# Storing weight gradients 1 MB at a time from common buffers in a four-pass attention kernel

## The chip, the cores and the metric

The kernel runs on one core of a Trainium2 chip. The metric is the device time of one execution in microseconds. Most kernels here were run five or six times, in rounds that alternate with runs of the kernel before on the same chip. A verdict of faster or slower needs 2%.

The engines by their names in the profile: PE (matrix multiply), PEld (its weight loads), DVE (vector), ACT (scalar), POOL (it issues the stores here), SP (it issues the loads here; "SPq" is its queue).

## The reference, cut to what matters

Two transformer layers are applied to one token, with the same weights used twice, and the gradients of all inputs are returned:

```python
x = x + attention(layernorm(x), k_cache, v_cache, wq, wo)   # 32 heads in 4 groups, 65,536 keys of 128
x = x + mlp(layernorm(x), w1, b1, w2, b2)                   # 1024 -> 3584 -> 1024, squared relu
# ... both once more; then the vector-Jacobian product with grad_out
```

The caches of K and V are 67 MB each. They are read four times (two forward passes, two backward passes), and gradients of the same size are written in the fourth pass. Each of the four weight gradients is a product of rank 2 (one term from each layer), 7.3 or 8.4 MB in bf16, 31 MB together. They too are made in the fourth pass, as background work.

## The kernel before

All loads and the K/V gradient stores use 11 common buffers ("slots") of 8 KB per partition, 1 MB each, reused in the order in which they are freed:

```python
FREE = deque(range(NSLOT))                     # NSLOT = 11
class Slot:
    def __init__(self):
        self.i = FREE.popleft()
        self.t = slotp.tile([P, BLK], BF, tag="slot%d" % self.i)     # BLK = 32 * 128
    def free(self):
        FREE.append(self.i)
```

The SP queue is in order: if the next load wants a buffer that is still in use, all loads behind it wait too. A pass is a pipeline over blocks of 8 key columns, and after each step the background gets a turn. First come the urgent generators (products of weight rows with a vector, which read 1 MB weight slabs through slots), then the normal ones (the weight gradients), which catch up with their schedule in a loop:

```python
def step(self, i):
    while self.urgent:
        if next(self.urgent[0][1], "end") == "end":
            self.urgent.popleft(); continue
        return
    want = self.total * (i - 2) / self.steps
    while self.normal and self.done < want:      # may run many times in one step
        ... next(self.normal[0]) ...; self.done += 1

def g_outer(pool, out_dram, nA, nB, a_cols, b_cols, c0=0):
    ...
    for ka in range(an):
        og = pool.tile([P, 8 * P], BF, name="og", tag="og", bufs=3)       # three buffers of 256 KB
        for n0 in range(0, bn * P, 512):
            pg = ps_gg()
            nc.tensor.matmul(pg[:, 0:nn], lhsT=ra[...], rhs=rb[...], start=True, stop=True)   # rank 2
            evac(og[:, n0:n0 + nn], pg[:, 0:nn], kind="f32")              # ACT or DVE
        nc.gpsimd.dma_start(out=out_dram[k * P:(k + 1) * P, ...], in_=og[...])
        yield
```

The tile `E` (64 KB per partition) holds the exponentials of both layers. The fourth pass reads it for the last time, from the last group to the first, and inside a group from the last column to the first.

## Time and profile before

| | before |
|---|---|
| median of 3 runs | 2097.63 us (2091.03 to 2101.38) |
| profiled run, span | 2109.1 us (2110.86 us as timed, longer than each of the three) |
| bytes moved | 803.55 MB, 381 GB/s on average |
| fourth pass, from its first V transpose (1265.6 us) to the end | 843.5 us |
| DMA idle in the fourth pass, by slices of 10 us from its start to the end of the span | 78.0 us |

From the page of the profile of before: the span; the granted TensorE clock in 40 slices of the span, in tenths of full speed; the busy share of the DMA engines in tenths; and GB/s in each slice.

```profile
span 2109.1 us, 69960 instructions
...
PEclk9999999579999987999999997859888888896897
DMA  9999999889999998999999996969989999999996
GB/s 381 418 416 417 417 415 403 315 323 412 408 411 418 415 369 322 375 412 416 415 419 416 384 328 233 370 233 395 390 338 422 404 394 371 420 389 375 386 411 280
```

For most of the first three passes DMA is at 9 tenths or more and moves 410 to 420 GB/s. Dips mark the dense stages between the passes. In the fourth pass (from the 25th slice) the rate falls to 233 twice and later to 338, 371 and 375, and the clock row dips with it.

Stretches of 10 us of before. The columns are the stretch, then busy us and the number of instructions of PE, PEld, DVE, ACT and POOL, then granted clock, DMA share and GB/s.

```profile
1360.00:1370.00 10.00, 7.38 (x62) 4.07 (x61) 5.35 (x18) 4.18 (x7) 2.16 (x4) 0.80 1.01 386
1370.00:1380.00 10.00, 5.16 (x35) 2.38 (x35) 4.17 (x8) 2.83 (x5) 1.62 (x3) 0.50 0.69 279
...
1390.00:1400.00 10.00, 6.58 (x32) 2.42 (x31) 4.31 (x13) 3.96 (x8) 1.62 (x3) 0.50 0.42 159
1400.00:1410.00 10.00, 10.00 (x53) 3.50 (x52) 3.99 (x7) 6.44 (x13) 1.86 (x4) 0.50 0.64 236
1410.00:1420.00 10.00, 10.00 (x59) 3.85 (x60) 6.00 (x11) 6.67 (x12) 1.37 (x3) 0.50 0.60 246
...
1450.00:1460.00 10.00, 9.34 (x146) 6.14 (x147) 8.98 (x18) 8.14 (x16) 2.15 (x4) 1.00 1.02 426
...
1470.00:1480.00 10.00, 8.46 (x98) 4.40 (x95) 6.28 (x12) 5.51 (x11) 1.61 (x3) 1.00 1.02 427
```

The stretches at 1450 and 1470 show what the pass can do: DMA share 1.02 and 426 GB/s. In the four slices shown between 1370 and 1420 DMA is at 0.42 to 0.69. PE is cold there (0.50): even where it is busy all the time (10.00) it gets through fewer than 60 matmuls in 10 us, against 146 at 1450. (Part of that is the mix: a burst of gradients brings more matmuls of 512 columns.)

From the list of waits of before over the fourth pass (us in total, times, longest us): ACT and DVE wait for a gradient store to land so that one of its three buffers comes free, and DVE once waits for a weight slab.

```profile
ACT og L144 <- DMA out_dram<-og: 64.6, 23, 7.0
DVE og L147 <- DMA out_dram<-og: 60.1, 21, 7.8
...
DVE mv_junk L345 <- DMA slot_32475<-in_A_wq_dram: 6.8, 1, 6.8
```

The chain of waits of before after 1500 us, summed by line:

```profile
by line: DMA out_dram<-og 22.6%; PE ps_gg L881 14.3%; PE ps_tr L818 12.3%; PE ps_gg L925 5.8%; PE ps_sc L837 5.1%; PE ps_acc L867 4.8%; issue 3.9%; PE ps_tr L849 3.2%; DMA slot_32475<-in_A_wq_dram 2.2%; DMA slot_42058<-in_A_k_cache_dram 2.0
```

Over a fifth of this chain is a gradient store ("out_dram<-og"). A store on the chain is not all loss, because DMA is also full much of that time.

### The profile page before, as it was taken

Reading aid. Unit: us, or ns where it says so; the run is one execution under the profiler, and the core shown is the slowest. Engines: PE = TensorE matmul, PEld = TensorE weight load, DVE = VectorE, ACT = ScalarE, POOL = GpSimd, SP = SyncE. Lnnn points to the kernel's source line nnn. Section 1 sums busy time; section 2 is a strip of 40 time slices with the busy share of each in tenths; the row PEclk is TensorE's granted clock in tenths of the full one; section 3 lists DMA queues with packets and bytes.
Section 4 is the critical chain, followed back from the end, with each engine's and each line's share of the span. In section 5 each row is a group of like instructions: output and inputs, shape, how many; then the busy total and the mean of one; then the engine's idle time right before and its main releaser. Section 6 shows DMA issues by size and latency. Waiting matters only on the chain.

```text
span 2109.1 us, 69960 instructions
## 1 busy us (share of the span) xinstructions
PE 1747.5 (83%) x31172; PEld 1368.0 (65%) x31172; DVE 1184.0 (56%) x2435; ACT 1121.9 (53%) x2029; POOL 139.6 (7%) x278
## 2 busy tenths in 40 slices
PE   6878787788888877888787797889788989888997
PEld 6777776787777776777677785535445554454553
DVE  3445444244444443834434367758667777686785
ACT  3545545144445452624334356647667766676775
POOL 0000000000000000000000000112111211111111
PEclk9999999579999987999999997859888888896897
DMA  9999999889999998999999996969989999999996
GB/s 381 418 416 417 417 415 403 315 323 412 408 411 418 415 369 322 375 412 416 415 419 416 384 328 233 370 233 395 390 338 422 404 394 371 420 389 375 386 411 280
DMA packets 148807, 803.55 MB, mean 381 GB/s; under 512 B 13964, under 2 KB 13978, under 8 KB 69274
## 3 DMA queue, kind: packets, MB, share of 16 engines
q1 hardware_dynamic: 120282, 633.39, 75.6%
q0 software_dynamic: 28224, 165.70, 19.3%
q8 instruction: 243, 3.98, 0.7%
q14 instruction: 58, 0.48, 0.1%
HBM read 633.35 MB, written 165.69 MB: 379 GB/s over the span
## 4 chain that ended last, share of the span: by engine, by line
PE 41%; DMA 34%; ACT 13%; DVE 8%; issue 3%; SPq 0%; ACTq 0%; POOL 0%; POOLq 0%; DVEq 0%
DMA out_dram<-og 9%; PE ps_gg L881 6%; PE ps_tr L566 6%; PE ps_tr L818 5%; ACT E L623 5%; PE ps_sc L584 4%; PE ps_tr L373 3%; PE ps_acc L650 3%; ACT kt L144 3%; DVE kt L147 3%; PE ps_gg L925 2%; PE ps_sc L837 2%; PE ps_acc L867 2%; PE ps_tr L849 1%; PE ps_bg L389 1%
## 5 line engine op out<-in xcount | busy, mean ns | idle before, releaser
L147 DVE COPY kt<-ps_tr 128x1024 bf16<-128x1024 bf16 x680 | 458.9, 687 | 342.7 <-PE ps_tr L566 157.5
L144 ACT COPY kt<-ps_tr 128x1024 bf16<-128x1024 bf16 x344 | 347.9, 1024 | 468.9 <-PE ps_tr L566 252.5
L584 PE MATMUL ps_sc<-L_qpad,kt 128*128 128x64 bf16 (+7 forms) x4096 | 196.0, 195 | 54.1 <-DVE kt L147 41.8
L584 PEld LDWEIGHTS <-kt 128*128 128x128 bf16 x4096 | 158.0, 100 | 73.4 <-DVE kt L147 50.3
L623 ACT ACTIVATE E<-S_sb,L_negm 128x128 bf16<-128x128 f32 x256 | 150.7, 988 | 26.5 <-DVE L_negm L619 26.5
L623 ACT ACTIVATION_READ_ACCUMULATOR E<-S_sb,L_negm 128x1 f32 x256 | 123.3, 482 | 0.0
L144 ACT CAST og<-ps_gg 128x512 bf16<-128x512 f32 x135 | 78.5, 593 | 79.6 <-DMA out_dram<-og 64.6
L837 PE MATMUL ps_sc<-DOB,kt 128*128 128x64 bf16 (+3 forms) x2048 | 119.6, 201 | 0.0
L147 DVE CAST og<-ps_gg 128x512 bf16<-128x512 f32 x105 | 72.0, 689 | 78.2 <-DMA out_dram<-og 60.1
L925 PE MATMUL ps_gg<-rowb,rowa 2*128 2x512 bf16 x240 | 93.0, 434 | 27.2 <-ACT og L144 17.6
L837 PEld LDWEIGHTS <-kt 128*128 128x128 bf16 x2048 | 95.4, 104 | 30.8 <-issue 29.0
L144 ACT COPY wt<-ps_tr 128x1024 bf16<-128x1024 bf16 (+1 forms) x60 | 57.6, 966 | 105.9 <-PE ps_tr L373 103.3
L729 PE MATMUL ps_sc<-dOpad,kt 128*128 128x64 bf16 (+7 forms) x2048 | 99.1, 194 | 15.5 <-ACT kt L144 11.8
L729 PEld LDWEIGHTS <-kt 128*128 128x128 bf16 x2048 | 76.5, 99 | 32.0 <-ACT kt L144 22.3
L589 DVE TENSOR_REDUCE pm_all<-S_sb 128x8 f32<-128x512 f32 x64 | 43.9, 686 | 91.7 <-ACT S_sb L588 91.6
L147 DVE COPY wt<-ps_tr 128x1024 bf16<-128x1024 bf16 (+1 forms) x92 | 59.7, 662 | 58.8 <-PE ps_tr L373 57.4
L881 PEld LDWEIGHTS <-xt 64*128 64x128 bf16 x1024 | 45.4, 95 | 65.3 <-issue 43.5
L928 POOL DMA_DIRECT2D out_dram<-og x124 | 67.3, 543 | 242.1 <-ACT og L144 104.7
L588 ACT COPY S_sb<-ps_sc 128x512 f32<-128x512 f32 x64 | 37.7, 589 | 82.6 <-PE ps_sc L584 82.4
L351 ACT ACTIVATE mv_t<-mv_t 128x1024 bf16<-128x1024 bf16 x56 | 59.3, 1060 | 24.6 <-DVE mv_t L350 24.5
L144 ACT COPY xt<-ps_tr 128x512 bf16<-128x512 bf16 x113 | 62.5, 596 | 11.0 <-PE ps_tr L849 10.4
L772 POOL COPY F_28535<-L_fw 128x128 f32<-128x128 f32 x2 | 0.6, 291 | 785.7 <-ACT L_fw L671 785.7
(2141 smaller groups left out, 3830.6 us busy)
## 6 DMA issues: line engine op xcount, KB each, us to landing
out_dram<-og POOLq DMA_DIRECT2D x116, 256.0 KB, 9.4
slot_171<-in_A_wq_dram SPq DMA_DIRECT2D x1, 1024.0 KB, 5.1
slot_205<-in_A_wq_dram SPq DMA_DIRECT2D x1, 1024.0 KB, 7.4
slot_245<-in_A_k_cache_dram SPq DMA_DIRECT2D x1, 1024.0 KB, 9.3
slot_292<-in_A_wq_dram SPq DMA_DIRECT2D x1, 1024.0 KB, 10.4
slot_329<-in_A_k_cache_dram SPq DMA_DIRECT2D x1, 1024.0 KB
slot_404<-in_A_wq_dram SPq DMA_DIRECT2D x1, 1024.0 KB
slot_441<-in_A_k_cache_dram SPq DMA_DIRECT2D x1, 1024.0 KB, 15.6
```

Source lines behind the costliest of these rows:

```text
L144: nc.scalar.copy(out=out, in_=in_)
L147: nc.vector.tensor_copy(out=out, in_=in_)
L373: nc.tensor.transpose(pt[:, i, :], slab[:, (q * w + i) * P:(q * w + i + 1) * P], ident_b[:, :])
L566: nc.tensor.transpose(pt[:, i, :], kb8[:, i, :], ident_b[:, :])
L584: nc.tensor.matmul(state["ps_s"][:, s:s + w, :].rearrange("p a b -> p (a b)"), lhsT=kt[:, i, :], rhs=L["qpad"][:, g, 0:w, :].rearrange("p ...
L623: nc.scalar.activation(out=E[:, g, c0:c0 + SU, L["lr"].start + h], in_=S[:, h, :], func=ACTF.Exp, bias=negm[:, g, su, h:h + 1], scale=SCAL ...
L729: nc.tensor.matmul(state["ps_dp"][:, s:s + w, :].rearrange("p a b -> p (a b)"), lhsT=vt[:, i, :], rhs=dOpad[:, g, 0:w, :].rearrange("p a b ...
L818: nc.tensor.transpose(pt[:, i, :], vb8[:, i, :], ident_b[:, :])
L837: nc.tensor.matmul(state["ps_dp"][:, s:s + w, :].rearrange("p a b -> p (a b)"), lhsT=vt[:, i, :], rhs=DOB[:, g, 0:w, :].rearrange("p a b - ...
L881: nc.tensor.matmul(pgs[h][:, :], lhsT=xt[t][64 * h:64 * h + 64, j1 // 8 + m, :], rhs=gg[64 * h:64 * h + 64, :, :].rearrange("p a b -> p (a ...
L925: nc.tensor.matmul(pg[:, 0:nn], lhsT=ra[:, ka * P:(ka + 1) * P], rhs=rb[:, n0:n0 + nn], start=True, stop=True)
L928: nc.gpsimd.dma_start(out=out_dram[k * P:(k + 1) * P, c0 + b0 * P:c0 + (b0 + bn) * P], in_=og[:, 0:bn * P])
```

## The change

The intent: gradients leave in 1 MB stores from the common buffers, at most one background step per pipeline step; halves of E become buffers once the fourth pass has used them; weight slabs are issued five steps before their use; a buffer whose store was just issued is "held back": it goes seven steps further back in the order of reuse; and memory is split as 12 buffers and 6 transposed weight tiles instead of 11 and 7.

```diff
-    NSLOT = 11
-    NWT = 7
+    STORE_STEPS = 7
+    WAIT_STEPS = 5
+    NSLOT = 12
+    NWT = 6
...
-            self.i = FREE.popleft()
+            self.i = heappop(FREE)[1]
...
-        def free(self):
-            FREE.append(self.i)
+        def free(self, stored=False):
+            NOW["step"] += 0.01
+            heappush(FREE, (NOW["step"] + (STORE_STEPS if stored else 0), self.i))
+    def add_slot(pool, tag):
+        SLOTS.append((pool, tag)); ...; heappush(FREE, (NOW["step"], len(SLOTS) - 1))
... # weight rows: the slab is issued by the for, then five steps pass
         for kc, slab in slab_it:
+            if kc % 4 == 0:
+                for _ in range(WAIT_STEPS if PS["pass4"] else 0):
+                    yield "wait"
... # background step: urgent "wait" lets normal work run; one normal step at most
+                if r == "wait":
+                    break
...
                     self.done += 1
+                    return
... # E in eight tiles; after its last use each is a buffer
+    def E_done(g, c0, n):
+        if c0 % EH == 0 and EH * R2 == BLK:
+            add_slot(epool, "E%d_%d" % (g, c0 // EH))
... # gradients
-                    og = pool.tile([P, 8 * P], BF, name="og", tag="og", bufs=3)
+            sl = Slot()
+            og = sl.t[:, :].rearrange("p (j n) -> p j n", j=4)
+            for j in range(4):
+                for n0 in range(0, 1024, 512):
+                    rank2(og[:, j, n0:n0 + 512], ra[:, bass.ds(j, P, step=4)], rb[:, n0:n0 + 512])
+                if j < 3:
+                    yield
+            nc.gpsimd.dma_start(out=out_dram[...].rearrange("(p j) n -> p j n", j=4), in_=og)
+            sl.free(stored=True)
```

The gradient of w1 (out_6) has its own form with rows of 7 KB, also one slot for each store. The gradient of wq still goes out in rows of 2 KB. The change also makes the gradient of wo before that of w1.

More of the change, by code (lines that the diff above doesn't have):

```diff
@@ L2 @@
 from collections import deque
+from heapq import heappush, heappop
 import concourse.bass as bass
@@ L211 @@
     BLK = J * DH
-    FREE = deque(range(NSLOT))
+    SLOTS = [(slotp, "slot%d" % i) for i in range(NSLOT)]
+    FREE = [(0, i) for i in range(NSLOT)]
+    NOW = {"step": 0}
     class Slot:
         def __init__(self):
-            self.i = FREE.popleft()
-            self.t = slotp.tile([P, BLK], BF, name="slot%d" % self.i, tag="slot%d" % self.i)
-        def free(self):
-            FREE.append(self.i)
+            self.i = heappop(FREE)[1]
+            pool, tag = SLOTS[self.i]
+            self.t = pool.tile([P, BLK], BF, name="slot", tag=tag)
+        def free(self, stored=False):
+            NOW["step"] += 0.01
+            heappush(FREE, (NOW["step"] + (STORE_STEPS if stored else 0), self.i))
+    def add_slot(pool, tag):
+        SLOTS.append((pool, tag))
+        NOW["step"] += 0.01
+        heappush(FREE, (NOW["step"], len(SLOTS) - 1))
     def kv_views(ap):
@@ L315, in bcast_vec @@
         nc.vector.tensor_copy(out=rows[0:nj, :], in_=pt[:, :])
-        vbc = pool.tile([P, nj * P], BF, name=tag, tag=tag)
+        vbc = pool.tile([P, nj * P], BF, name=tag, tag=tag, bufs=1)
         for j0 in range(0, nj, 4):
@@ L333, in g_rowdots @@
         n = nj * P
-        vbc = bcast_vec(vcol, nj, mvs, "vbc")
         y = vec.tile([P, nk], F32, name=name)
         nc.gpsimd.memset(y[:], 0.0)
-        yield
+        vbc = None
         L = load
         for kc, slab in slab_it:
+            if kc % 4 == 0:
+                for _ in range(WAIT_STEPS if PS["pass4"] else 0):
+                    yield "wait"
+            if vbc is None:
+                vbc = bcast_vec(vcol, nj, mvs, "vbc")
+                yield
             a = (L["dve"] + 0.10 + n * 0.00105, L["act"])
@@ L437, in step @@
             while self.urgent:
-                if next(self.urgent[0][1], "end") == "end":
+                r = next(self.urgent[0][1], "end")
+                if r == "end":
                     self.urgent.popleft()
                     continue
+                if r == "wait":
+                    break
                 return
-            want = self.total * (i - 2) / self.steps
-            while self.normal and self.done < want:
+            while self.normal and self.done < self.total * (i - 2) / self.steps:
                 if next(self.normal[0], "end") == "end":
@@ L468, in pipeline @@
             bg.step(i)
+            NOW["step"] += 1
     def new_layer(name, lay):
@@ L482, in new_layer, with E @@
         return L
-    E = epool.tile([P, G, C, R2], BF, name="E")
+    EH = max(SU, C // 2)
+    ETILE = {}
+    for g in range(G):
+        for h in range(C // EH):
+            ETILE[(g, h)] = epool.tile([P, EH * R2], BF, name="E", tag="E%d_%d" % (g, h))
+    def E(g, c0, n):
+        h, c = divmod(c0, EH)
+        return ETILE[(g, h)][:, :].rearrange("p (c r) -> p c r", r=R2)[:, c:c + n, :]
+    def E_done(g, c0, n):
+        if c0 % EH == 0 and EH * R2 == BLK:
+            add_slot(epool, "E%d_%d" % (g, c0 // EH))
     def gsl(g):
@@ L622, in stats @@
             for h in range(R):
-                nc.scalar.activation(out=E[:, g, c0:c0 + SU, L["lr"].start + h], in_=S[:, h, :], func=ACTF.Exp,
+                nc.scalar.activation(out=E(g, c0, SU)[:, :, L["lr"].start + h], in_=S[:, h, :], func=ACTF.Exp,
                                      bias=negm[:, g, su, h:h + 1], scale=SCALE, accum_out=rs[:, h:h + 1])
@@ L649, in v8 @@
                 w = min(8, (su + 1) * SU - c)
-                nc.tensor.matmul(ps_o[:, 0:w, :], lhsT=vb8[:, i, :], rhs=E[:, g, c:c + w, lr],
+                nc.tensor.matmul(ps_o[:, 0:w, :], lhsT=vb8[:, i, :], rhs=E(g, c, w)[:, :, lr],
                                  start=(c % SU == 0), stop=(c % SU == SU - 1), skip_group_check=True)
@@ L734, in vS @@
                 nc.vector.tensor_tensor(out=dsT[:, :, :], in0=state["ps_dp"][:, :, :],
-                                        in1=E[:, g, c0:c0 + HB, L["lr"]], op=ALU.mult)
+                                        in1=E(g, c0, HB)[:, :, L["lr"]], op=ALU.mult)
                 add_load(dve=0.7)
@@ L842, in vS @@
                 X = dspool.tile([P, J, R2], BF, name="X", tag="X")
-                nc.vector.tensor_tensor(out=X[:, :, :], in0=ps_dp[:, :, :], in1=E[:, g, c0:c0 + J, :], op=ALU.mult)
+                nc.vector.tensor_tensor(out=X[:, :, :], in0=ps_dp[:, :, :], in1=E(g, c0, J), op=ALU.mult)
                 add_load(dve=0.13 + J * R2 * 0.00105)
                 xt = []
-                for src in (X[:, :, :], E[:, g, c0:c0 + J, :]):
+                for src in (X[:, :, :], E(g, c0, J)):
                     pt2 = ps_tr()
@@ L852, in vS @@
                     xt.append(xx)
+                E_done(g, c0, J)
                 state[("X", g, c0 // J)] = (X, xt)
@@ L888, in k8 @@
                 nc.gpsimd.dma_start(out=(GVv if t else GKv)[g][b], in_=stg)
-                state.pop("st").free()
+                state.pop("st").free(stored=True)
             if c8 == sulast[(g, su)]:
@@ L896, in attn_bwd4, with rows2 @@
         pipeline(items, [(vT, 0), (vS, TLEAD), (k8, B4_LAG)], bg)
-    def rows2(pool, cols, j0, jn, tag):
-        cc = pool.tile([P, 8, 2], BF, name="r2_cc", tag="r2_cc", bufs=2)
+    def rows2(cols, j0, jn, rows):
+        cc = tmp.tile([P, 4, 2], BF, name="r2_cc")
         for l in range(2):
             nc.vector.tensor_copy(out=cc[:, 0:jn, l], in_=cols[l][:, j0:j0 + jn])
-        rows = pool.tile([2, 8 * P], BF, name=tag, tag=tag)
-        for k0 in range(0, jn, 4):
-            kn = min(4, jn - k0)
-            pg = ps_gg()
-            for jj in range(kn):
-                nc.tensor.matmul(pg[0:2, jj * P:(jj + 1) * P], lhsT=cc[:, k0 + jj, :], rhs=ident_b[:, :], start=True, stop=True)
-            evac(rows[0:2, k0 * P:(k0 + kn) * P], pg[0:2, 0:kn * P], kind="f32")
-        return rows
@@ L912, in g_outer @@
-    def g_outer(pool, out_dram, nA, nB, a_cols, b_cols, c0=0):
-        for b0 in range(0, nB, 8):
-            bn = min(8, nB - b0)
-            rb = rows2(pool, b_cols, b0, bn, "rowb")
-            for a0 in range(0, nA, 8):
-                an = min(8, nA - a0)
-                ra = rows2(pool, a_cols, a0, an, "rowa")
-                yield
-                for ka in range(an):
-                    og = pool.tile([P, 8 * P], BF, name="og", tag="og", bufs=3)
-                    for n0 in range(0, bn * P, 512):
-                        nn = min(512, bn * P - n0)
-                        pg = ps_gg()
-                        nc.tensor.matmul(pg[:, 0:nn], lhsT=ra[:, ka * P:(ka + 1) * P], rhs=rb[:, n0:n0 + nn], start=True, stop=True)
-                        evac(og[:, n0:n0 + nn], pg[:, 0:nn], kind="f32")
-                    k = a0 + ka
-                    nc.gpsimd.dma_start(out=out_dram[k * P:(k + 1) * P, c0 + b0 * P:c0 + (b0 + bn) * P], in_=og[:, 0:bn * P])
-                    yield
@@ L931, in n_outer, with rank2 @@
-    def n_outer(nA, nB):
-        return (nA + -(-nA // 8)) * -(-nB // 8)
+        pg = ps_gg()
+        for jj in range(jn):
+            nc.tensor.matmul(pg[0:2, jj * P:(jj + 1) * P], lhsT=cc[:, jj, :], rhs=ident_b[:, :], start=True, stop=True)
+        evac(rows, pg[0:2, 0:jn * P], kind="f32")
+    def rank2(out, ra, rb):
+        pg = ps_gg()
+        n = out.shape[-1]
+        nc.tensor.matmul(pg[:, 0:n], lhsT=ra, rhs=rb, start=True, stop=True)
+        evac(out, pg[:, 0:n], kind="f32")
+    def g_outer(pool, out_dram, nA, nB, a_cols, b_cols, c0=0):
+        rb = pool.tile([2, 8 * P], BF, name="rowb", tag="rowb")
+        for k in range(0, nB, 4):
+            rows2(b_cols, k, 4, rb[0:2, k * P:(k + 4) * P])
+            yield
+        for a0 in range(0, nA, 4):
+            ra = pool.tile([2, 4 * P], BF, name="rowa", tag="rowa", bufs=2)
+            rows2(a_cols, a0, 4, ra[0:2, :])
+            yield
+            sl = Slot()
[4 more added lines that the diff above has]
+                if j < 3:
+                    yield
+            nc.gpsimd.dma_start(out=out_dram[a0 * P:(a0 + 4) * P, c0:c0 + 1024].rearrange("(p j) n -> p j n", j=4), in_=og)
+            sl.free(stored=True)
+            yield
@@ new lines, in g_outer_wide @@
+    def g_outer_wide(pool, out_dram, nA, nB, a_cols, b_cols):
+        rsl = Slot()
+        rb = rsl.t
+        for k in range(0, nB, 4):
+            rows2(b_cols, k, 4, rb[0:2, k * P:(k + 4) * P])
+            yield
+        for a in range(nA):
+            if a % 4 == 0:
+                ra = pool.tile([2, 4 * P], BF, name="rowa", tag="rowa", bufs=2)
+                rows2(a_cols, a, 4, ra[0:2, :])
+                yield
+            sl = Slot()
+            for n0 in range(0, nB * P, 512):
+                rank2(sl.t[:, n0:n0 + 512], ra[:, (a % 4) * P:(a % 4 + 1) * P], rb[0:2, n0:n0 + 512])
+                if n0 % 1024 == 512:
+                    yield
+            nc.gpsimd.dma_start(out=out_dram[a * P:(a + 1) * P, :], in_=sl.t[:, 0:nB * P])
+            sl.free(stored=True)
+            yield
+        rsl.free()
@@ L935, with n_outer @@
+    def n_outer(nA, nB, wide=False):
+        return nB // 4 + nA // 4 + nA * (-(-nB // 8)) if wide else nB // 4 + nA // 4 * 5
     psA_stack = ExitStack()
@@ L1113 @@
     bg.normal.append(g_outer(bgpool, out_8, FC, DC, [L4["g"], L2["g"]], [gx, dx2]))
-    bg.normal.append(g_outer(bgpool, out_6, DC, FC, [L4["n"], L2["n"]], [dh4, dh2]))
     bg.normal.append(g_outer(bgpool, out_5, HQ, DC, [L3["oT"], L1["oT"]], [dx3, dx1]))
-    bg.total = n_outer(FC, DC) + n_outer(DC, FC) + n_outer(HQ, DC) + (G - 1) * n_outer(DC, DC)
+    bg.normal.append(g_outer_wide(bgpool, out_6, DC, FC, [L4["n"], L2["n"]], [dh4, dh2]))
+    bg.total = n_outer(FC, DC) + n_outer(DC, FC, True) + n_outer(HQ, DC) + (G - 1) * n_outer(DC, DC)
     bg.steps = len(ITEMS[3]) - 4
```

## The prediction

> **What bounds it now.** By stretches of 10 us, the first three passes over the caches are bound by DMA: between the dense stages its share is 1.01, at 412 to 418 GB/s; the change hardly touches them. The fourth pass (1280 to 2109 us) moves 306 MB in 830 us, 369 GB/s. Its 24 clean slices (granted clock 1.0, DMA 0.99 or more, PE over 9 of 10 us) move 415 GB/s and run 133 matmuls per 10 us; at those rates its 306 MB need 738 us and its 8,419 recorded matmuls 631 us. So DMA is the floor there, and 90 us are lost:
>
> 1. Idle DMA: the shares sum to 771 us of 830. 21 us are lost between 1370 and 1430, some 20 us around 1490, 1530 to 1570, 1750, 1850 and 1940: after the urgent row products have held the background back, several 256 KB gradient rows are emitted in one step into three buffers. In the list of waits ACT and DVE wait 43 and 40 us after 1520 us for a store of og; the chain of waits after 1500 us gives 22.6% to it. PE goes cold meanwhile: in the 38 slices with a clock under 0.9 DMA averages 338 GB/s. The Trainium skill (TensorE: Matmul & The Clock Gate, Part 1) says that an idle window halves the clock; the trace agrees, 0.50 to 0.67 in these stalls.
> 2. Single waits: 13.6 us for a weight slab, 9 us twice for a V block, 12.3 us for the last K block; the DMA queue waited 14 to 19 us four times after 1520 us for a K/V gradient store whose buffer the next load wanted.
> 3. Small stores: 30 MB of gradients leave in 2 KB pieces; slices full of them move 290 GB/s at a DMA share of 0.87, 335 at full share against 420: an estimated 15 to 20 us. The skill (DMA: Bandwidth & Descriptors, Rules for kernel authors) asks for 1 MiB per DMA.
>
> **What the change does.** The same 240 rank-2 matmuls and evictions (0.6 us on ACT, 0.69 on DVE) come at most two per step, so bursts go. Two of four gradient families leave in 8 KB pieces, one in 7 KB, one stays at 2 KB. Slabs get five steps (16 us) between issue and use. Buffers: 11 become 12, and each used half of E adds one, up to 20. In program order, loads into a stored buffer come 10 or more steps after the store (before: 6 to 11). Costs: gradients take slots, so in the first quarter some loads reuse a buffer freed only 4 to 5 steps earlier (before: mostly 9); the transposed-weight queue shrinks from 7 to 6.
>
> **Sum.** Idle in the body of pass four: 43 us, I expect 30 back; small stores 14 us; slab and V waits, beyond that overlap, 10 us; tail 3 us; one more slot across three dense stages 4 us. About 60 us, all on the critical path because DMA is the bound and it idles.
>
> **Predicted: 2037 us**, 2014 to 2068 for 8 in 10. Faster by over 2% (under 2055.7): 0.77; within: 0.21; slower: 0.02.
>
> **What would show it.** Waits of ACT and DVE on gradient stores near zero; no slice under 0.8 DMA share between 1350 and 1450; granted clock near 1 in pass four; pass four at 395 GB/s or more, about 775 us; passes one to three unchanged; slab waits under 4 us.
>
> **What would make it wrong.** Loads in the first quarter of pass four starve because gradients hold slots; a 1 MB store lands so late that the queue blocks on its buffer; PE stays cold for other reasons.

## The result and the profile after

The changed kernel took 2048.69 us (median of 4 runs, 2046.51 to 2050.70), against 2096.57 us of before in the same rounds. The ratio is 0.9772, with a 95% interval of 0.9746 to 0.9799: 2.3% faster. A ratio here is the mean time of one kernel's fast runs over that of the other's fast runs of the same rounds, so it is not quite the ratio of the medians. Run again later, it gave 2048.01 us and a ratio of 0.9769.

The page after, the same rows as before:

```profile
span 2046.9 us, 69658 instructions
...
PEclk9999999679999997999999999788889998996997
DMA  9999999999999998999999995999999998999997
GB/s 380 419 415 418 415 415 419 371 333 411 415 413 417 416 415 324 371 409 415 417 417 415 419 352 193 349 391 401 423 398 415 412 418 338 416 424 397 368 423 325
```

Fourth-pass slices now mostly run at 390 to 424 GB/s. From its first V transpose (1250.1 us) the fourth pass takes 796.8 us, and 795.0 us in the profile of the second set, against 843.5 us before: 47 to 49 us less. (The profiled execution of before was slower than the timed ones, so a part of this may be chance.) DMA idles 46.7 and 41.5 us in it instead of 78.0. The pass still began 15 us earlier than in the profile of before, but that is mostly chance. Across the 14 profiles it begins between 1247 and 1266 us; one experiment with the first three passes of before (one row per step, below) begins it at 1249.9, as early as the changed kernel.

Stretches of the changed kernel:

```profile
1240.00:1250.00 10.00, 7.81 (x170) 6.79 (x166) 7.50 (x33) 3.43 (x4) 0.51 (x1) 1.00 0.30 90
1250.00:1260.00 10.00, 8.56 (x116) 6.64 (x116) 5.33 (x18) 5.44 (x8) 0.56 (x2) 0.83 0.38 133
1260.00:1270.00 10.00, 9.65 (x158) 6.69 (x156) 9.16 (x17) 7.11 (x14) 0.57 (x1) 1.00 0.25 102
...
1350.00:1360.00 10.00, 10.00 (x73) 4.88 (x71) 6.69 (x12) 7.09 (x13) 1.07 (x2) 0.50 1.01 419
1360.00:1370.00 10.00, 9.88 (x123) 5.82 (x121) 8.12 (x16) 7.07 (x14) 1.07 (x2) 0.87 1.03 426
1370.00:1380.00 10.00, 9.09 (x119) 5.44 (x118) 9.19 (x23) 8.18 (x16) 1.07 (x2) 1.00 1.02 426
...
1390.00:1400.00 10.00, 9.15 (x120) 5.59 (x118) 9.80 (x20) 8.37 (x16) 0.88 (x2) 1.00 1.01 423
...
1410.00:1420.00 10.00, 9.69 (x87) 5.53 (x87) 6.36 (x11) 5.52 (x11) 1.60 (x3) 0.50 1.01 424
...
1690.00:1700.00 10.00, 8.47 (x58) 3.74 (x58) 4.31 (x7) 3.30 (x6) 0.53 (x1) 0.51 0.57 238
1700.00:1710.00 10.00, 9.92 (x100) 5.88 (x98) 6.47 (x12) 6.44 (x12) 0.53 (x1) 0.63 0.76 244
```

The hole around 1370 to 1420 is gone: at 1370 there are 426 GB/s at a full clock where before had 279 at 0.50. The clock is not full throughout: at 1350 and 1410 it is 0.50, and yet DMA is full (1.01). So a cold PE does not by itself make DMA run dry.

Three weak places remain. At the start of the pass (1240 to 1290) DMA idles about 25 us while PE and DVE are busy. Seven blocks kept from the third pass need no load, there is little to store yet, and the load queue stands 21.6 us in two waits until DVE has done with a weight slab; which of these matters is not shown. At 1690 to 1710 PE is cold. The rest is the tail.

Waits of the changed kernel over the fourth pass, first those of the engines, then of the load queue:

```profile
PE ps_tr L853 <- DMA slot<-in_A_v_cache_dram: 34.7, 7, 12.3
...
PE ps_acc L903 <- DMA slot<-in_A_k_cache_dram: 22.8, 4, 7.9
...
DVE slot L150 <- DMA out_dram<-slot: 8.5, 1, 8.5
```

```profile
SPq L250 <- DMA out_dram<-slot: 438.8, 73, 17.1
```

The waits of ACT and DVE for a gradient store fell from 125 us together to 8. No wait of DVE for a slab is left. The load queue, on the other hand, now waits 439 us in K/V loads for stores to leave a buffer (148 us in 16 waits before). That is not a loss by itself: DMA is full most of that time. PE waits 35 and 23 us for V and K. The chain of waits by line (here from 1280 to 2050 us) agrees: the gradient store is gone from the top, and loads have taken its place.

```profile
by line: DMA slot<-in_A_v_cache_dram 14.5%; PE ps_tr L853 13.2%; PE ps_gg L917 12.9%; ACT slot L147 8.7%; PE ps_gg L947 8.2%; DMA slot<-in_A_k_cache_dram 7.6%; PE ps_sc L872 5.6%; PE ps_acc L903 5.1%; PE ps_tr L884 3.5%; DMA out_dram<-slot 
```

### The profile page after: what moved, and what is told of

The parts are those of the page before. It is cut to its first block, busy times and chain, and to the rows that moved or that the text cites. A ratio compares the mean times of both kernels' runs of the same rounds, so it can differ in the third digit from the quotient of the medians.

```text
span 2046.9 us, 69658 instructions
## 1 busy us (share of the span) xinstructions
PE 1694.8 (83%) x31148; PEld 1335.8 (65%) x31148; DVE 1180.9 (58%) x2470; ACT 1117.5 (55%) x2023; POOL 90.5 (4%) x185
## 4 chain that ended last, share of the span: by engine, by line
PE 41%; DMA 32%; ACT 15%; DVE 8%; issue 3%; SPq 0%; POOLq 0%; ACTq 0%; DVEq 0%
DMA slot<-in_A_v_cache_dram 16%; DMA slot<-in_A_k_cache_dram 12%; PE ps_tr L601 5%; PE ps_tr L853 5%; ACT E L658 5%; PE ps_gg L917 5%; PE ps_sc L619 4%; ACT slot L147 4%; ACT kt L147 3%; PE ps_tr L391 3%; PE ps_acc L685 3%; PE ps_gg L947 3%; DVE kt L150 3%; PE ps_sc L872 2%; PE ps_acc L903 2%
## 5 line engine op out<-in xcount | busy, mean ns | idle before, releaser
L147 ACT CAST slot<-ps_gg 128x512 bf16<-128x512 f32 x752 | 407.5, 595 | 184.9 <-PE ps_gg L917 156.0
L150 DVE CAST slot<-ps_gg 128x512 bf16<-128x512 f32 x519 | 340.9, 685 | 84.9 <-PE ps_gg L917 48.7
L601 PE MATMUL ps_tr<-ident_b,slot 128*128 128x128 bf16 x4096 | 296.2, 226 | 19.6 <-DMA slot<-in_A_k_cache_dram 17.1
L601 PEld LDWEIGHTS <-slot 128*128 128x128 bf16 x4096 | 249.7, 102 | 23.4 <-DMA slot<-in_A_k_cache_dram 19.1
L853 PEld LDWEIGHTS <-slot 128*128 128x128 bf16 x2048 | 129.6, 102 | 178.2 <-issue 135.6
L853 PE MATMUL ps_tr<-ident_b,slot 128*128 128x128 bf16 x2048 | 199.6, 232 | 35.7 <-DMA slot<-in_A_v_cache_dram 34.7
L619 PEld LDWEIGHTS <-kt 128*128 128x128 bf16 x4096 | 158.2, 100 | 74.0 <-DVE kt L150 52.3
L685 PE MATMUL ps_acc<-E,slot 128*128 128x64 bf16 (+4 forms) x4096 | 168.1, 197 | 25.2 <-issue 7.3
L744 PE MATMUL ps_tr<-ident_b,slot 128*128 128x128 bf16 x2048 | 146.2, 226 | 24.8 <-DMA slot<-in_A_v_cache_dram 23.9
L685 PEld LDWEIGHTS <-slot 128*128 128x128 bf16 x4096 | 145.9, 101 | 27.1 <-issue 23.1
L744 PEld LDWEIGHTS <-slot 128*128 128x128 bf16 x2048 | 122.9, 101 | 41.1 <-DMA slot<-in_A_v_cache_dram 40.1
L903 PE MATMUL ps_acc<-X,slot 128*128 128x64 bf16 (+3 forms) x2048 | 115.2, 197 | 22.8 <-DMA slot<-in_A_k_cache_dram 22.8
L903 PEld LDWEIGHTS <-slot 128*128 128x128 bf16 x2048 | 85.2, 101 | 57.2 <-issue 33.1
L872 PE MATMUL ps_sc<-DOB,kt 128*128 128x64 bf16 (+3 forms) x2048 | 113.8, 197 | 0.0
L872 PEld LDWEIGHTS <-kt 128*128 128x128 bf16 x2048 | 91.1, 102 | 20.4 <-issue 20.3
## 6 DMA issues: line engine op xcount, KB each, us to landing
out_dram<-slot POOLq DMA_DIRECT2D x151, 1024.0 KB, 11.1
slot<-in_A_wo_dram SPq DMA_DIRECT2D x32, 1024.0 KB, 11.1
```

The costliest lines, as they stand in the source:

```text
L147: nc.scalar.copy(out=out, in_=in_)
L150: nc.vector.tensor_copy(out=out, in_=in_)
L601: nc.tensor.transpose(pt[:, i, :], kb8[:, i, :], ident_b[:, :])
L619: nc.tensor.matmul(state["ps_s"][:, s:s + w, :].rearrange("p a b -> p (a b)"), lhsT=kt[:, i, :], rhs=L["qpad"][:, g, 0:w, :].rearrange("p ...
L685: nc.tensor.matmul(ps_o[:, 0:w, :], lhsT=vb8[:, i, :], rhs=E(g, c, w)[:, :, lr], start=(c % SU == 0), stop=(c % SU == SU - 1), skip_group_ ...
L744: nc.tensor.transpose(pt[:, i, :], vb8[:, i, :], ident_b[:, :])
```

## The experiments

Twelve kernels ran, all correct. Time medians are given with the ratio to before in the same rounds; different calls used different chips, so compare ratios. "Fourth pass" is from its first V transpose to the end of the span, in the one profiled execution.

| kernel | median us | ratio (95%) | fourth pass us | DMA idle in it us |
|---|---|---|---|---|
| after | 2048.69 | 0.9772 (0.9746 to 0.9799) | 796.8 | 46.7 |
| after again | 2048.01 | 0.9769 (0.9733 to 0.9805) | 795.0 | 41.5 |
| after, background may catch up in bursts | 2059.72 | 0.9825 (0.9803 to 0.9847) | 796.6 | 43.7 |
| before, one row per step | 2068.90 | 0.9860 (0.9834 to 0.9885) | 810.4 | 49.4 |
| after, 11 buffers and 7 weight tiles | 2072.58 | 0.9882 (0.9856 to 0.9908) | 813.1 | 52.1 |
| after, E not reused | 2095.82 | 0.9999 (0.9978 to 1.0021) | 841.3 | 65.2 |
| after, slabs not fetched ahead | 2056.85 | 0.9817 (0.9780 to 0.9854) | 806.9 | 48.9 |
| after, stored buffers not held back | 2064.18 | 0.9842 (0.9802 to 0.9882) | 803.4 | 54.3 |
| after, 1 MB stores in 2 KB pieces | 2048.99 | 0.9776 (0.9737 to 0.9815) | 789.1 | 35.6 |
| after, last gradient ahead of the last rows | 2052.68 | 0.9793 (0.9754 to 0.9833) | 793.7 | 40.5 |
| after, small rows in own buffers (11 buffers) | 2081.36 | 0.9935 (0.9900 to 0.9969) | 824.9 | 60.3 |
| after, gradients start 32 steps later | 2057.84 | 0.9816 (0.9788 to 0.9845) | 800.6 | 51.1 |
| small rows, no hold-back, no fetch-ahead | 2065.50 | 0.9882 (0.9847 to 0.9917) | 821.9 | 57.8 |

A difference of ratios times about 2095 us is the difference in time; 0.001 is 2.1 us. What follows rests on the ratios and their intervals. Idle is counted from the first V transpose to the end of the span.

### Bursts put back into the changed kernel

```diff
                     self.done += 1
-                    return
```

> The changed kernel with the limit of one background step per pipeline step taken away again, so that after the urgent row products the background catches up in one go. Theory A (bursts are the cost, because they hold up ACT, DVE and PE and let DMA run dry): 2060 to 2070 us against 2048, with slices of DMA share under 0.8 back between 1330 and 1440 us. Theory B (the buffers are the cost: three small buffers made engines wait for stores, and a burst into the common buffers harms nobody): within 4 us of the changed kernel.

Measured: 0.9825 against 0.9769 and 0.9772, so about 11 us lost, at the near edge of theory A. But theory A's mark was not seen: no slice between 1330 and 1440 fell under 0.96 of DMA, and the fourth pass of the profiled execution (the fastest of the five) took 796.6 us like the changed kernel's. This is the slice with the least DMA share:

```profile
1360.00:1370.00 10.00, 10.00 (x67) 4.61 (x64) 5.25 (x9) 5.61 (x10) 1.06 (x2) 0.50 0.96 361
```

Its profile lost 8 us ahead of the fourth pass, which began at 1258.2 us, where the two programs are the same. The timed runs say that bursts still cost something; where is left open.

### One row per step in the kernel before

```diff
                 else:
                     self.done += 1
+                    return
```

> The kernel before with one thing of the change alone: at most one background step (one 256 KB row) per pipeline step. Theory A (bursts): most of the gain in the fourth pass, 2065 to 2075 us against 2097, and the waits of ACT and DVE for a gradient store fall below 20 us together. Theory B (buffers and their order are the cost): 2088 us or more, waits for K/V gradient stores in the DMA queue stay.

Measured: 2068.90 us, ratio 0.9860, so 29 us of the 48 from one line. The fourth pass took 810.4 us instead of 843.5. Its waits for gradient stores over the fourth pass:

```profile
ACT og L144 <- DMA out_dram<-og: 51.0, 26, 4.6
...
DVE og L147 <- DMA out_dram<-og: 38.4, 17, 4.9
```

They fell from 65 and 60 us to 51 and 38, much less than expected, and the longest fell from 7.8 to 4.9 us. Most of the fall lies where the hole of before was: between 1360 and 1440 us the two sums are 30.1 us before and 8.3 us here. The weakest slices left there are these:

```profile
1390.00:1400.00 10.00, 9.09 (x73) 4.40 (x73) 5.28 (x9) 5.94 (x12) 2.15 (x4) 0.66 0.96 356
...
1430.00:1440.00 10.00, 9.92 (x71) 4.98 (x69) 4.57 (x8) 5.03 (x9) 1.39 (x4) 0.50 0.75 285
```

DMA idles 49.4 us in the pass instead of 78.0, which is also 29 us. So the gain is shown, and that DMA idles less with it. Whether the waits cost by their clusters, which let PE go cold, or by their sum, which fell by 35 us, these two profiles do not tell.

### The old split of memory in the changed kernel

```diff
-    NSLOT = 12
-    NWT = 6
+    NSLOT = 11
+    NWT = 7
```

> The changed kernel with the old split of memory, 11 buffers and 7 transposed weight tiles. The prediction's term (one more buffer is worth 4 us over three dense stages): 2052 us. Rival, read from the two profiles (the fourth pass began 15 us earlier after the change, 12 of them gained in the first dense stage): 2060 us or more, and the profile shows the fourth pass beginning at 1260 us or later. If the 12 us were the luck of the clock in one profile, the time stays under 2054.

Measured: 2072.58 us, ratio 0.9882: the twelfth buffer, at the price of one weight tile, is worth about 24 us, six times the term in the prediction. It does not act where the prediction or the rival put it. The fourth pass began at 1252.0 us, as early as after; it took 813.1 us instead of 795 to 797. Over all profiles the pass began on average at 1257 us in the five kernels with 11 buffers and at 1254 us in the nine with 12, less than the spread of either. In the list of waits of the 11-buffer kernel two waits for weight slabs are back, which the changed kernel does not have, and PE waits 57 us for V instead of 35 and 38 (for K less: 3.5 us instead of 23 and 13):

```profile
PE ps_tr L853 <- DMA slot<-in_A_v_cache_dram: 57.0, 13, 9.1
PE ps_tr L391 <- DMA slot<-in_A_wq_dram: 10.8, 1, 10.8
DVE mv_t L368 <- DMA slot<-in_A_wo_dram: 5.9, 1, 5.9
```

### Used halves of E not reused

```diff
-                E_done(g, c0, J)
```

> The changed kernel without turning used halves of E into buffers, so 12 buffers to the end. Theory A (DMA bound, prefetch by 12 buffers is nearly enough): up to 2056 us. Theory B (gradients hold buffers, loads starve without the eight more): 2065 us or more, with the loss in the second half of the fourth pass.

Measured: 2095.82 us, ratio 0.9999. Without the halves of E the whole gain is gone, although one background step per pipeline step, 1 MB stores, 12 buffers, hold-back and fetch-ahead are all still there. The loss begins in the first half already (fourth slice of 40 us of the pass: 358 GB/s against 423) and is largest between 1690 and 1770 us (327 and 298 GB/s in two such slices). Stretches of that kernel:

```profile
1660.00:1670.00 10.00, 4.16 (x43) 2.91 (x44) 1.98 (x3) 1.54 (x3) 0.00 (x0) 0.52 1.01 418
1670.00:1680.00 10.00, 9.57 (x151) 5.99 (x148) 9.20 (x23) 7.56 (x15) 1.10 (x3) 1.00 1.02 422
1680.00:1690.00 10.00, 9.34 (x139) 6.05 (x138) 8.32 (x18) 8.20 (x15) 1.20 (x3) 1.00 0.92 303
1690.00:1700.00 10.00, 5.46 (x73) 3.37 (x72) 8.00 (x15) 6.33 (x12) 0.89 (x2) 1.00 1.01 422
1700.00:1710.00 10.00, 9.84 (x83) 5.13 (x81) 4.69 (x7) 5.44 (x9) 0.53 (x1) 0.52 1.00 406
1710.00:1720.00 10.00, 10.00 (x74) 5.03 (x71) 5.76 (x11) 5.32 (x10) 0.53 (x1) 0.50 0.85 331
1720.00:1730.00 10.00, 10.00 (x77) 5.07 (x74) 5.42 (x9) 5.01 (x8) 0.53 (x1) 0.50 0.42 152
```

At 1680 PE runs 139 matmuls at a full clock. At 1690 DMA is full (1.01) and PE is busy only 5.46 of 10 us: it waits 4.0 us for a V load. After that the clock is 0.50 and PE is busy all the time at half speed, with fewer than 85 matmuls in 10 us, and now it is DMA that runs dry (0.85, then 0.42). Stores are issued 8 to 10 us apart there, against 4 to 6 us between 1670 and 1696, and between 1700 and 1735 the load queue waits 18.9 us for them. So this short starvation seems to be paid twice. The order in time is shown; that the slow clock is the link was not tested alone, and it is no rule: the longer wait for V before it (9.3 us, at 1660) was followed by a full clock and full DMA at 1670.

### No fetch-ahead of slabs

```diff
-    WAIT_STEPS = 5
+    WAIT_STEPS = 0
```

> The changed kernel with weight slabs used at once after their issue (no five steps of waiting). The prediction's term (slab waits 10 us): 2056 to 2060 us, and DVE waits of 5 us and more for slabs come back. Rival, read from the profile of the changed kernel (at the start of the fourth pass the load queue waited 18 us for a buffer that a slab held through its five steps, with DMA shares of 0.25 to 0.4): waiting costs as much at the start as it gains later, so the time stays within 5 us, and the DMA shares between 1240 and 1290 us rise.

Measured: 2056.85 us, ratio 0.9817 against 0.9769: about 10 us, as the prediction had it, though the two intervals overlap. In its profile a DVE wait for a slab is back:

```profile
DVE mv_t L368 <- DMA slot<-in_A_wq_dram: 8.2, 1, 8.2
```

The rival falls: the DMA shares at the start of the pass stayed low (0.19, 0.31, 0.55 in the three stretches from 1250), so that idle time is not made only by slabs that sit in a buffer through their five steps.

### Stored buffers not held back

```diff
-    STORE_STEPS = 7
+    STORE_STEPS = 0
```

> The changed kernel with buffers reused in the order in which they are freed, without the seven steps that hold back a buffer whose store was just issued. If loads queue behind unfinished stores: 2058 us or more, waits of the load queue for stores rise above the 439 us of the changed kernel, and PE waits for K and V loads rise above 58 us. If DMA is simply full and a waiting queue costs nothing: within 4 us.

Measured: 2064.18 us, ratio 0.9842, about 15 us lost. The load queue's waits for stores in K/V loads:

```profile
SPq L250 <- DMA out_dram<-slot: 452.1, 57, 27.4
```

The sum is only a little higher (452 us against 439 and 431), but the longest single wait is 27.4 us instead of 17.1, and DMA idles 54 us instead of 42 to 47. The expected rise of PE's waits for K and V did not come (42 us against 58 and 51), but PE once waits 9.0 us for a weight slab. The time sides with the first theory; how the longer waits turn into lost time is not shown.

### The same stores in 2 KB pieces

The four row blocks of a store lie one behind the other in DRAM instead of interleaved, so each partition writes four pieces of 2 KB instead of one of 8 KB.

```diff
-  rank2(og[:, j, n0:n0 + 512], ra[:, bass.ds(j, P, step=4)], ...)
+  rank2(og[:, j, n0:n0 + 512], ra[:, j * P:(j + 1) * P], ...)
-  ....rearrange("(p j) n -> p j n", j=4), in_=og)
+  ....rearrange("(j p) n -> p j n", j=4), in_=og)
```

> The changed kernel with the same 1 MB stores, but two gradient families (15.7 MB) written in 2 KB pieces instead of 8 KB ones. The prediction's term (2 KB pieces cost 15 to 20 us for 30 MB at 335 against 420 GB/s, so about 9 us for these): 2055 to 2060 us, about 5,900 more packets. Rival (the low rate of the slices with small stores came from stalled engines, not from the pieces): within 3 us.

Measured: 2048.99 us, ratio 0.9776: nothing. The store queue of the changed kernel (run again) and of this one (packets, MB, time as a share of 16 engines over the span):

```profile
q0 software_dynamic: 24048, 165.70, 19.5%
```

```profile
q0 software_dynamic: 25968, 165.70, 19.6%
```

The packets rose by 1,920, not by the 5,900 expected, and the share by 0.1 points. The sizes in the packed traces tell why: 3,840 packets of 4 KB took the place of 1,920 of 8 KB. The gradients of before left in 4 KB packets too (7,680, all 31 MB); none of 2 KB is recorded among its stores. So for these 15.7 MB this run puts back the packets that before had. The prediction's term for small pieces is refuted for these 15.7 MB. That the low rates it was read from belong to stalled engines is then the likely reading; it was not tested by itself.

### The changed kernel again

> The changed kernel as it is, for a comparison on the same chip as the next three. All theories: 2045 to 2052 us. Its profile also shows whether the start of the fourth pass (1250 us in its first profile, 1258 in the one with bursts, 1266 in the profile of before) moves from one execution to the next with the same program.

Measured: 2048.01 us, ratio 0.9769. The fourth pass began at 1253.5 us, and took 795.0 us.

### The last gradient ahead of the last row product

```diff
+    run(gwq(lastg[3]))
     rows = Rows(bufs=2)
 ...
-    run(gwq(lastg[3]))
```

> The changed kernel with the last group's weight gradient (2 MB) put ahead of the last row product and the layer norm at the end, so that its last 1 MB store is in flight while those run. In the profile the last store is issued at 2039.3 us and the span ends at 2046.9. If the tail is this store: 4 to 6 us less, 2042 to 2044 us. If the chain of PE and DVE work at the end sets it: within 2 us.

Measured: 2052.68 us, ratio 0.9793, not to be told from the changed kernel. Relative to the start of the pass, the last 1 MB store was issued 784 us after it instead of 789, but the store of dx0 now came last. No version that beats the changed kernel was found.

### Small rows in own buffers, with all the rest

The gradients' code of before (three buffers of 256 KB, one row per background step) was put into the changed kernel. With those buffers only 11 slots and 7 weight tiles fit, so the fair partner is the 11-buffer kernel above.

```diff
-    NSLOT = 12
-    NWT = 6
+    NSLOT = 11
+    NWT = 7
-            sl = Slot()                                 # 1 MB stores
...
+                    og = pool.tile([P, 8 * P], BF, name="og", tag="og", bufs=3)
...
```

> The changed kernel with its gradients put back into three own 256 KB buffers and stored row by row, which forces 11 buffers and 7 weight tiles; one row per step, used halves of E, fetch-ahead and the order of reuse stay. Compare with the 11-buffer kernel with 1 MB stores (2072.6 us against 2098.6). Theory C (gradients in the common buffers are a cost, which the halves of E pay back; the size of a store gives nothing): 2040 to 2060 us, at least 12 us faster than that kernel. Theory D (1 MB stores from common buffers are a gain of their own): 2075 us or slower.

Measured: 2081.36 us, ratio 0.9935. Theory C falls; the result is in the range of theory D. But it is also slower than before with one row per step alone (0.9860), which has neither the halves of E nor the other aids. So something in the aids harms this kernel, and one more run was needed before D could be believed.

### Small rows without hold-back and fetch-ahead

```diff
-    STORE_STEPS = 7
-    WAIT_STEPS = 5
+    STORE_STEPS = 0
+    WAIT_STEPS = 0
```

> The kernel with small row stores and used halves of E (2081.4 us) without the seven steps that hold a stored buffer back and without the five steps of fetch-ahead: that is one row per step (2068.9 us by itself) plus the halves of E, 11 buffers at the start. If holding stored buffers back is what harms a kernel that is short of buffers, and the halves of E help by themselves: 2050 to 2065 us. If the halves of E give nothing to small rows: 2066 to 2072 us. If it is 2078 us or more, neither order nor fetch-ahead was what made the kernel with small rows slow.

Measured: 2065.50 us, ratio 0.9882. Two things follow. Hold-back and fetch-ahead together cost this kernel about 11 us (0.9935 against 0.9882, on different chips, with intervals that just overlap), while each of them gained 10 to 15 us in the changed kernel. And the halves of E gave nothing to small rows: 0.9882 with them, 0.9860 without. Theory D stays open. With hold-back and fetch-ahead in both, 1 MB stores are about 11 us faster than rows in own buffers, at 11 buffers each (0.9882 against 0.9935); with the two aids taken from the rows alone, they tie at 0.9882. The missing fourth kernel, 1 MB stores with 11 buffers and without the aids, was not run.

### Gradients start later

```diff
-  while self.normal and self.done < self.total * (i - 2) / self.steps:
+  while self.normal and self.done < self.total * (i - 34) / (self.steps - 32):
```

> The changed kernel with the background gradients starting 32 pipeline steps later, when the first half of E has become a buffer. If gradients in the first quarter starve the loads: 4 to 10 us less, 2038 to 2044 us, and more loads in flight before 1360 us. If DMA or the engines are full later on, the work only moves: within 3 us, or slower if steps get crowded at the end.

Measured: 2057.84 us, ratio 0.9816, about 9 us slower, though the intervals overlap. A gain from a later start is ruled out, so gradients in the first quarter do not starve the loads by enough to matter. That the same work is in the way later on is the likely reason; it is not shown.

## Why the prediction was right or wrong, point by point

The predicted time was 2037 us (2014 to 2068) and the measured 2048.69 us. Direction, range and the place of the gain (the fourth pass) were right. The sum was 60 us and the result 48, and the terms differ more than the total. That the total came so near is partly luck: the 14 us for larger pieces and the 3 us at the tail did not come, and a buffer priced at 4 us gave about 24.

- **DMA is the floor of the fourth pass, and it idles.** Right. The gain of 47 to 49 us in the pass goes with 31 to 37 us less idle DMA.
- **30 us from the end of bursts.** Right, and shown for the kernel before: that one line gains 29 us, with 29 us less idle DMA. Taken out of the changed kernel it costs only 11.
- **14 us from larger pieces.** Wrong. The same bytes in 2 KB pieces (4 KB packets, as before had) cost nothing. This is the step that failed: "335 at full share against 420" took the rate of stretches, in which engines stalled as well, for the cost of a piece.
- **10 us from slab and V waits.** Right in size for the slabs: about 10 us when the fetch-ahead is undone, with intervals that overlap. The slab waits are under 4 us, as predicted. The V waits did not go but rose: PE's transposes wait 35 us for V after, against 16 before (9.5, 4.7 and 2.1 us in its list).
- **3 us from the tail.** Not seen. From the last K matmul to the end of the span it is 26 us before (2083 to 2109) and 25.5 us after (2021.4 to 2046.9).
- **4 us from one more slot, in the dense stages.** Wrong in size and place. It is worth about 24 us, in the fourth pass; the dense stages show at most 3 us, within chance.
- **Halves of E.** The prediction listed them and gave them no term. Without them nothing is left of the gain. The cost they pay for was listed too, "gradients take slots", also without a number.
- **Marks.** Waits of ACT and DVE for gradient stores fell from 125 to 8 us (right). No slice under 0.8 between 1350 and 1450 (right). Passes one to three unchanged (right). The clock near 1: wrong; 27 of the 10 us slices of the pass are under 0.9, against 39 before. Fourth pass at 395 GB/s and 775 us: it came to 385 GB/s (306.7 MB in 796.8 us). The 775 us were counted from 1280 us, 14 us after the first V transpose of that profile.
- **A warning that came near.** "PE stays cold for other reasons" was named. Of the cold slices that remain some go with idle DMA, such as 1690 in the changed kernel; others, such as 1350 and 1410, do not.

So the gain is best told like this. Pacing alone gives 29 us. Moving the gradients into the common buffers is not shown to give anything by the size of its stores: with as many buffers as before, the full change stands at 0.9882, no better than pacing alone (0.9860). But it frees the memory of the three row buffers, and with one weight tile less that makes the twelfth buffer, 24 us. (The kernel before with 12 buffers and 6 tiles does not build: a pool of the fourth pass needs 11.1 KB per partition, and 3.8 KB are left.) In this form the gradients draw on the common buffers: without the halves of E none of the gain is left, and without the order of reuse that keeps loads from standing behind a fresh store 15 us of it are lost. The parts do not add up: undone singly in the changed kernel they are worth 11, 24, 47, 10 and 15 us, 107 in all, against 48 for the whole.

## What to carry to other kernels

Pace background work to one small piece per pipeline step before enlarging its stores: one line did 60% of this gain. Price a buffer in the stage where DMA and PE are both near their limits; a starvation there can be followed, as at 1690 without the halves of E, by stretches at half clock in which DMA idles as well. Do not read the cost of small pieces off a stretch in which engines stall: keep the stores and change the pieces alone.

## What the Trainium skill lacked or had wrong

- "DMA: Bandwidth & Descriptors", Rules for kernel authors, asks for 1 MiB per DMA for bandwidth. For stores beside other traffic the runs here leave it open: with 11 buffers, 256 KB stores without hold-back and fetch-ahead tie with 1 MB stores that have both (0.9882 each), and with both they are slower (0.9935). Inside 1 MB stores, 2 KB against 8 KB pieces give 0.9776 against 0.9769.
- The same page, in its anatomy of one DMA, gives about 2 us plus bytes over 436 GB/s for a DMA issued from GpSimd, an estimated 4.4 us for 1 MB. It has no time from issue to landing on a loaded core. In the changed kernel the median is 11.1 us for 1 MB stores, issued from GpSimd, and 17.0 us for K loads and 19.0 us for V loads, issued from SP; lead times for buffers in this kernel have to be planned with those.
- "TensorE: Matmul & The Clock Gate", Part 1, says that about 3.4 us of sustained work release the throttle. In the kernel without the halves of E, PE was busy 10.00 of 10 us in two stretches running (1710 to 1730) at a granted clock of 0.50. The page does warn that its clock records have been seen stuck, but the matmul counts (74 and 77 in 10 us) agree with a slow clock: 139 at a full clock 30 us earlier in the same kernel. So do matmuls of one shape (64x512), with a mean of 609 ns there and 381 ns at 1680 to 1690. Whether a stream with so many transposes and rank-2 products is sustained work in the page's sense, no run here tells.
- The same page says that the number of slow matmuls at the start of one kernel varies from run to run. No page gives the size of this for a dense stage amid DMA-bound work. Here, with nearly the same program ahead of it, the fourth pass began anywhere from 1247 to 1266 us. The granted clock from 395 to 425 us was 0.50 in four of the five profiles that began it last (1258.0 to 1266.0 us) and 0.67 to 0.90 in the other ten; that the clock makes the difference is read from this and not tested.
